# Four broadcast vectors out of four column tiles of one PSUM bank, with the order of all engines written anew

## The chip, the cores and the metric

The kernel runs on one core of one Trainium2 chip. The metric is the device time of one execution in microseconds (us); of several runs the median counts. The profiled execution and the plain runs are the same program.

## The reference, cut to what matters

A transformer block whose norms and residuals are modulated by a conditioning vector, on x of 2048 tokens by 512:

```python
mod = (silu(c) @ w_mod).reshape(1, 6, 1, 512)          # c: (1, 512)
sa, ca, ga, sb, cb, gb = mod[:, 0], ..., mod[:, 5]
h = layernorm(x) * (1 + ca) + sa
x = x + ga * A(h)      # 32 heads of 16, window of 256 tokens, qkv and output projections
h = layernorm(x) * (1 + cb) + sb
x = x + gb * B(h)      # layernorm, token-mixing MLP: 2048 -> 1792, gelu, 1792 -> 2048
```

Six vectors of 512 numbers come out of one small product. `sa` and `ca` are wanted along the partitions (`modFM`). The other four, `ga`, `cb`, `sb`, `gb`, are wanted as tiles of 128 equal rows, since tokens or MLP columns lie on the partitions where they are used: `bc_ga`, `bc_cb1` (cb + 1), `bc_sb`, `bc_gb`. These four are the subject here.

## The kernel before, in words

**Work.** The sequence is worked in four groups of 512 tokens. Of each group, queries, keys and values are projected (`pq`, `pk`, `pv`), heads are attended, the output is projected (`pa`, pieces named `wo`), added to x and normed twice (`l2`, `l3`) to give `hb`. Attention goes by 75 chunks: a score group on TensorE (`S`, names `pss` and `psb`), two exponentials on ScalarE (`et<-pss`, then `et<-psb`), masks on VectorE (`et<-et,maskt`), and on TensorE three pieces of weighted and plain sums (`po`, pieces named `AV`). `pss` has one buffer: the next score group waits for the exponential that reads it. The first MLP product runs in partial sums beside the last attention chunks (pieces `p`, names `pu`, `part`), the rest of it (`u`) after them, then the second product (`py`) and the output.

**Pieces.** Dense products are cut into pieces of two matmuls of 512 columns. A piece is emitted at full width, or as four column tiles of 32 columns of weights each (the helper `mm`); the scheduler picks the second where few dense pieces stand between sums (`NEAR_RUN`), so that TensorE need not change its tiling.

**Evictions.** Results in PSUM are taken out by VectorE or ScalarE (`qe` queries, `ke` keys, `ve` values, `pe` partial sums). [...]

**Order.** Nothing is left to run-time choice. `ops` lists all operations with their engines; `ORDER` is a table of numbers, the sequence in which they are emitted, and each engine runs its own in that sequence. `CHOSEN` names the operations that go to another engine than their first. `Ordered` pins the instructions of each queue, SyncE's transfers among them: an instruction that waits holds up all behind it on its queue.

**The place of the change.** `sT` is silu(c), four columns of 128. `sT_rep` spreads it to 4 x 128 equal columns, so that a matmul with it as weights gives 128 equal rows. For each of the four vectors `e_bc` runs four full-width matmuls of 512 columns into a bank of its own, and `e_bce` evicts that bank on VectorE into the tile, with the factor `ZSCALE` for `ga` and plus one for `cb`. `mod_ops` collects what must be done before the output projection: the four evictions, the MLP biases (`b12`, from the transfers `bl`) and the scaling of the output weights by `bc_ga` (`wod`). The loads of MLP weights (`w1`) wait for all of them too.

## Time and profile before

| | us |
|---|---|
| median of 3 runs | 258.86 |
| lowest and highest run | 256.61, 259.86 |
| time of the profiled execution | 257.62 |
| its span, first to last instruction | 255.8 |
| TensorE busy in the span | 240.1 |
| VectorE, ScalarE, GpSimd busy | 205.5, 172.8, 134.2 |
| TensorE's granted clock | 1.0 throughout |

The profiled execution takes 1.8 us more than its span, for what lies before the first and after the last instruction. Busy times are unions over an engine's instructions; matmuls overlap each other in the pipeline, so TensorE's figure is an upper one. Nearly all instructions carry line 254, that of the recording helper, so groups are told apart by the names of their tiles: `out<-in`.

### The profile page before, as it was taken

Reading aid. Unit: us, or ns where it says so; the run is one execution under the profiler, and the core shown is the slowest. Engines: PE = TensorE matmul, PEld = TensorE weight load, DVE = VectorE, ACT = ScalarE, POOL = GpSimd, SP = SyncE. Lnnn points to the kernel's source line nnn. Section 1 sums busy time; section 2 is a strip of 40 time slices with the busy share of each in tenths; the row PEclk is TensorE's granted clock in tenths of the full one; section 3 lists DMA queues with packets and bytes.
Section 4 is the critical chain, followed back from the end, with each engine's and each line's share of the span. In section 5 each row is a group of like instructions: output and inputs, shape, how many; then the busy total and the mean of one; then the engine's idle time right before and its main releaser. Section 6 shows DMA issues by size and latency. Waiting matters only on the chain.

```text
span 255.8 us, 11463 instructions
## 1 busy us (share of the span) xinstructions
PE 240.1 (94%) x5125; PEld 137.7 (54%) x5125; DVE 205.5 (80%) x378; ACT 172.8 (68%) x288; POOL 134.2 (52%) x220
## 2 busy tenths in 40 slices
PE   7999988999889889997999898999999999999995
PEld 3666655656656555655566455557444444444443
DVE  5599998999989979989798879898977974444443
ACT  4699998999998999997899898988207620000000
POOL 6069938967597599969787679964000000000000
PEclk9999999999999999999999999999999999999999
DMA  6998340381032100000621913401699901111111
GB/s 200 327 351 279 68 26 3 82 128 49 3 67 44 27 3 5 4 6 3 177 77 46 249 44 85 122 8 45 179 347 393 352 24 44 41 41 42 60 44 41
DMA packets 39657, 26.44 MB, mean 103 GB/s; under 512 B 11960, under 2 KB 35512, under 8 KB 39608
## 3 DMA queue, kind: packets, MB, share of 16 engines
q1 hardware_dynamic: 39600, 25.71, 35.4%
q8 instruction: 40, 0.66, 1.1%
q14 instruction: 9, 0.07, 0.1%
q10 hardware_dynamic: 8, 0.00, 0.0%
HBM read 22.03 MB, written 2.10 MB: 94 GB/s over the span
## 4 chain that ended last, share of the span: by engine, by line
PE 68%; DVE 16%; ACT 7%; issue 3%; DMA 2%; SPq 2%; POOL 1%; ACTq 0%
PE py L254 19%; PE pu L254 18%; PE po L254 8%; PE pss L254 7%; ACT et L254 7%; DVE et L254 5%; PE pa L254 4%; PE pk L254 3%; PE pq L254 3%; PE pv L254 3%; DVE h L254 2%; DMA x<-in_A_x_dram 2%; DVE st L254 2%; SPq L254 2%; DVE kb L254 2%
## 5 line engine op out<-in xcount | busy, mean ns | idle before, releaser
L254 ACT ACTIVATE et<-pss 128x1536 bf16<-128x1536 f32 (+2 forms) x90 | 101.5, 1147 | 12.0 <-PE psb L254 8.0
L254 PE MATMUL py<-guT,w2r 128*128 128x512 bf16 (+2 forms) x238 | 48.5, 366 | 0.0
L254 ACT ACTIVATE et<-psb 128x512 bf16<-128x512 f32 (+2 forms) x90 | 43.6, 508 | 0.0
L254 DVE TENSOR_TENSOR et<-et,maskt 128x2048 bf16<-128x2048 bf16 (+2 forms) x38 | 42.1, 1120 | 0.4 <-ACT et L254 0.4
L254 PEld LDWEIGHTS <-KT 32*128 32x128 bf16 (+1 forms) x1856 | 24.4, 97 | 30.4 <-issue 26.0
L254 PE MATMUL pu<-hb,w1s 128*32 128x512 bf16 (+1 forms) x260 | 38.8, 380 | 0.8 <-DVE part L254 0.7
L254 PE MATMUL pss<-QT,KT 32*64 32x32 bf16 (+7 forms) x1392 | 34.8, 202 | 4.8 <-ACT et L254 2.2
L254 PE MATMUL po<-et,VT 128*32 128x256 bf16 (+2 forms) x960 | 33.4, 234 | 3.8 <-DVE vb L254 2.2
L254 PEld LDWEIGHTS <-w2r 128*128 128x128 bf16 x238 | 22.8, 98 | 25.9
L254 PE MATMUL psb<-QT,KT 32*128 32x224 bf16 (+3 forms) x464 | 34.3, 203 | 0.9 <-issue 0.9
L254 PE MATMUL po<-et,ones_bd 128*32 128x256 bf16 (+3 forms) x624 | 31.4, 269 | 0.5 <-issue 0.5
L254 DVE TENSOR_TENSOR otile<-py,xr 128x512 bf16<-128x512 f32 (+2 forms) x17 | 11.2, 660 | 24.6 <-PE py L254 24.5
L254 POOL TENSOR_SCALAR KT<-kb,mask_par 128x512 bf16<-128x512 bf16 (+1 forms) x30 | 21.1, 714 | 13.2 <-DVE kb L254 11.8
L254 PEld LDWEIGHTS <-VT 128*32 128x32 bf16 x960 | 21.7, 96 | 10.8 <-issue 3.8
L254 DVE BATCH_NORM_STATS2 st<-x 128x6 f32<-128x512 bf16 x32 | 21.3, 680 | 2.0 <-DMA x<-in_A_x_dram 1.9
L254 POOL TENSOR_SCALAR VT<-vb,mask_half 128x512 bf16<-128x512 bf16 x25 | 20.1, 810 | 4.9 <-DVE vb L254 4.4
L254 PEld LDWEIGHTS <-w1s 128*32 128x32 bf16 (+1 forms) x260 | 13.9, 97 | 14.5 <-issue 1.2
L254 PE MATMUL pk<-h1T,wqkv 128*32 128x512 bf16 (+4 forms) x222 | 20.7, 333 | 0.0
L254 PEld LDWEIGHTS <-wqkv 128*32 128x32 bf16 (+1 forms) x380 | 15.2, 96 | 8.8 <-issue 1.1
L254 PE MATMUL pu<-hb,w1r 128*128 128x512 bf16 (+1 forms) x84 | 18.0, 380 | 0.0
L254 PE MATMUL pv<-wqkv,h1T 128*32 128x256 bf16 x512 | 17.6, 274 | 0.1
L254 PE MATMUL pa<-wod,OT 128*32 128x512 bf16 (+1 forms) x130 | 16.7, 381 | 0.2 <-DVE x L254 0.2
(107 smaller groups left out, 365.3 us busy)
## 6 DMA issues: line engine op xcount, KB each, us to landing
w2r<-in_B_w_dram SPq DMA_DIRECT2D x14, 512.0 KB, 10.5
w1s<-in_B_w_dram SPq DMA_DIRECT2D x19, 256.0 KB, 3.3
w1r<-in_B_w_dram SPq DMA_DIRECT2D x9, 256.0 KB, 4.9
x<-in_A_x_dram SPq DMA_DIRECT2D x16, 128.0 KB, 4.9
wmod<-in_w_mod_dram SPq DMA_DIRECT2D x4, 512.0 KB, 8.5
out_dram<-otile SPq DMA_DIRECT2D x15, 128.0 KB, 1.7
wmod<-in_w_mod_dram SPq DMA_DIRECT2D x4, 256.0 KB, 3.4
wqkv<-in_A_wqkv_dram SPq DMA_DIRECT2D x4, 256.0 KB, 5.2
```

The source lines that it names most:

```text
L254: ins = call(*args, **kwargs)
```

## The change

`sT_rep` keeps 32 equal columns instead of 128. One bank takes all four vectors: for each k the four matmuls write rows 0-31, 32-63, 64-95 and 96-127 from four column tiles. One eviction `bce` brings the bank to `bcs`, with a scale and an addend per partition (`bc_fix`: `ZSCALE` on the rows of `ga`, one added on the rows of `cb`). Four transfers on SyncE's queue (`bb`) then read the 32 rows of a vector four times over and fill the 128 rows of its tile. `ORDER` and `CHOSEN` are new tables.

```diff
 ORDER = [
-    2, 6, 0, 1, 7, 39, 8, 5, 40, 3, 9, 41, 10, 4, 42, 38, 11, 43, 13, 44, 45, 14, 46, 15, 47, 18, 16, 17, 20, 50, 48,
+    2, 6, 0, 1, 33, 7, 34, 8, 5, 35, 3, 9, 36, 10, 4, 37, 11, 38, 13, 39, 40, 14, 41, 15, 18, 42, 16, 20, 17, 19, 45,
...
 CHOSEN = {
...
-    sT_rep = modw.tile([P, ND, P], BF, name="sT_rep")
+    sT_rep = modw.tile([P, ND, 32], BF, name="sT_rep")
+    bcs = modw.tile([P, D], BF, name="bcs")
+    bc_fix = modw.tile([P, 2], F32, name="bc_fix")
+    nc.gpsimd.memset(bc_fix[:, 0:1], 1.0)
+    nc.gpsimd.memset(bc_fix[0:32, 0:1], ZSCALE)
+    nc.gpsimd.memset(bc_fix[:, 1:2], 0.0)
+    nc.gpsimd.memset(bc_fix[32:64, 1:2], 1.0)
...
-    o_rep = op("sTrep", "DVE", 0.35, lambda e: ve.tensor_copy(
-        out=sT_rep[:], in_=sT[:].unsqueeze(2).to_broadcast([P, ND, P])), deps=[o6], pos=-6, ready=15.0)
+    o_rep = op("sTrep", "DVE", 0.2, lambda e: ve.tensor_copy(
+        out=sT_rep[:], in_=sT[:].unsqueeze(2).to_broadcast([P, ND, 32])), deps=[o6], pos=-6, ready=15.0)
...
     mod_ops = []
-    for n, (v, dst) in enumerate(((2, bc_ga), (4, bc_cb1), (3, bc_sb), (5, bc_gb))):
-        def e_bc(n, v=v):
...
-                te.matmul(
-                    box["bc", v][:], lhsT=sT_rep[:, k, :], rhs=wmod[:, k, v * D : (v + 1) * D],
-                    start=(k == 0), stop=(k == ND - 1),
-                )
...
-        a, z = dense(f"bc{v}", [0.435] * 2, e_bc, [o_rep], 9.0 + n, cls="D", alloc="od", ready=22.0)
-        b = op(f"bce{v}", "DVE", 0.6, e_bce, deps=[z], pos=9.0 + n)
+    vectors = ((2, bc_ga), (4, bc_cb1), (3, bc_sb), (5, bc_gb))
+
+    def e_bc(n):
+        if n == 0:
+            box["bc"] = bank([P, D], F32, "ps_b")
+        for k in (2 * n, 2 * n + 1):
+            for i, (v, _) in enumerate(vectors):
                 te.matmul(
+                    box["bc"][32 * i : 32 * i + 32, :], lhsT=sT_rep[:, k, :], rhs=wmod[:, k, v * D : (v + 1) * D],
+                    start=(k == 0), stop=(k == ND - 1), tile_position=(0, 32 * i), skip_group_check=True,
                 )
...
+    def e_bce(e):
+        ve.tensor_scalar(
+            out=bcs[:], in0=box["bc"][:], scalar1=bc_fix[:, 0:1], scalar2=bc_fix[:, 1:2], op0=ALU.mult, op1=ALU.add,
+        )
...
+    for n, (v, dst) in enumerate(vectors):
+        def e_bb(e, n=n, dst=dst):
+            dma.dma_start(out=dst[:], in_=bcs[32 * n : 32 * n + 32, :].unsqueeze(1).to_broadcast([32, ND, D]))
+
+        mod_ops.append(op("bb", "SP", 0.65, e_bb, deps=[bce], pos=9.0 + n, extra=1.0))
```

What the tables move shows at three places.

VectorE, from the spreading of silu(c) to the first evictions of the vectors. Before (`ps_b` is the bank of a vector; `pk`, `pv` banks of projections, `et` exponentials):

```order
L254 COPY sT_rep<-sT 128x512
L254 CAST vb<-pv 128x512
L254 TENSOR_TENSOR et<-et,maskt 128x4x128
L254 TENSOR_TENSOR et<-et,maskt 128x4x64
L254 TENSOR_SCALAR KT_1_156<-kb,mask_par 128x8x32 x2
L254 TENSOR_TENSOR et<-et,maskt 128x8x64 x2
L254 CAST bc_gb<-ps_b 128x512
```

After the change:

```order
L253 COPY sT_rep<-sT 128x128
L253 TENSOR_TENSOR et<-et,maskt 128x4x128
L253 TENSOR_TENSOR et<-et,maskt 128x4x64
L253 CAST vb<-pv 128x512
L253 CAST kb<-pk 128x256
L253 CAST QT_1_148<-pk 128x256
L253 TENSOR_SCALAR KT_1_156<-kb,mask_par 128x8x32 x2
L253 TENSOR_TENSOR et<-et,maskt 128x8x64 x2
L253 TENSOR_TENSOR et<-et,maskt 128x4x128
L253 TENSOR_TENSOR et<-et,maskt 128x4x64
L253 CAST vb<-pv 128x512
L253 TENSOR_SCALAR bcs<-ps_b,bc_fix 128x512
```

One eviction stands a little later than the first of the four stood; the evictions of `bc_sb`, `bc_ga` and `bc_cb1` that followed it before are gone.

SyncE's queue behind the loads of x, before:

```order
L254 DMA_TRANSPOSE h1T_181<-xn 128x4x128 x4
L254 DMA b1b<-in_B_b_dram 128x14x1
L254 DMA b2b<-in_B_b_dram 128x16x1
L254 DMA w1s_1856<-in_B_w_dram 128x4x256
L254 DMA_TRANSPOSE h1T_180<-xn 128x4x128 x4
```

After the change:

```order
L253 DMA_TRANSPOSE h1T_181<-xn 128x4x128 x4
L253 DMA bc_gb<-bcs 128x1x512
L253 DMA bc_cb_118<-bcs 128x1x512
L253 DMA bc_ga<-bcs 128x1x512
L253 DMA bc_sb<-bcs 128x1x512
L253 DMA b1b<-in_B_b_dram 128x14x1
L253 DMA b2b<-in_B_b_dram 128x16x1
L253 DMA_TRANSPOSE h1T_180<-xn 128x4x128 x4
L253 DMA w1s_1957<-in_B_w_dram 128x4x256
```

The four transfers stand between the transposes of the second token group and the biases; the transposes of the third group now stand ahead of the first load of MLP weights instead of behind it.

ScalarE from the twelfth to the fifteenth chunk, before (`lz` are the logarithm and the reciprocal of the sums):

```order
L254 ACTIVATE et<-pss 128x3x2x256
L254 ACTIVATE et<-psb 128x2x256
L254 ACTIVATE lz<-lz 128x256
L254 ACTIVATE et<-pss 128x12x32 x2
L254 ACTIVATE lz<-po 128x256
L254 ACTIVATE et<-psb 128x4x32 x2
L254 ACTIVATE et<-pss 128x3x2x256
L254 ACTIVATE lz<-lz 128x256
L254 ACTIVATE et<-psb 128x2x256
L254 ACTIVATE et<-pss 128x3x2x256
```

After the change:

```order
L253 ACTIVATE et<-pss 128x3x2x256
L253 ACTIVATE et<-psb 128x2x256
L253 ACTIVATE vb<-pv 128x512
L253 ACTIVATE lz<-po 128x256
L253 ACTIVATE et<-psb 128x2x256
L253 ACTIVATE lz<-lz 128x256
L253 ACTIVATE et<-pss 128x12x32 x2
L253 ACTIVATE QT_1_152<-pq 128x512
L253 ACTIVATE et<-psb 128x4x32 x2
L253 ACTIVATE et<-pss 128x3x2x256
L253 ACTIVATE QT_0_151<-pq 128x512
L253 ACTIVATE et<-psb 128x2x256
```

Three evictions of projections (`vb`, twice `QT`) stand between the exponentials on ScalarE where none stood; they were VectorE's.

## The prediction

> **What bounds the kernel now.** I read the page's first two parts, then the chain of work that ended last, then busy time by stage.

> ```profile
> PE 240.1 (94%) x5125; PEld 137.7 (54%) x5125; DVE 205.5 (80%) x378; ACT 172.8 (68%) x288; POOL 134.2 (52%) x220
> PE   7999988999889889997999898999999999999995
> ACT  4699998999998999997899898988207620000000
> PE 68%; DVE 16%; ACT 7%; issue 3%; DMA 2%; SPq 2%; POOL 1%; ACTq 0%
> ```

> TensorE is on the chain for 68% of the span and wholly at the end; ScalarE is nearly full in the first 27 slices and then falls away. So there are two regimes, and I cut the span at the start of every tenth chunk, which is the start of its `et<-pss` exponential in ScalarE's timeline. First and last of these 75:

> ```profile
> 10.94 1.45 ACT L254 ACTIVATE et<-pss 128x1536 bf16<-128x1536 f32 x1 [0.73 <-PE pss L254]
> 173.32 1.44 ACT L254 ACTIVATE et<-pss 128x1536 bf16<-128x1536 f32 x1
> ```

> Busy time in these stretches (chunks 0-9, 10-19, and so on; then the tail of `u` pieces and the stretch of `py`); the columns are the length, then TensorE, weight loads, VectorE, ScalarE, GpSimd:

> ```profile
> 10.94:33.61 22.67, 21.59 (x564) 14.78 (x564) 22.08 (x53) 22.13 (x37) 16.69 (x32) 1.00 0.80 231
> 33.61:55.21 21.60, 19.33 (x665) 12.96 (x665) 20.61 (x40) 20.20 (x34) 15.01 (x24) 1.00 0.37 41
> 55.21:75.16 19.95, 18.73 (x588) 12.24 (x590) 18.41 (x31) 19.68 (x33) 15.49 (x26) 1.00 0.28 63
> 75.16:97.35 22.19, 19.28 (x684) 12.42 (x677) 20.71 (x35) 20.00 (x34) 17.70 (x26) 1.00 0.11 22
> 97.35:118.03 20.68, 20.08 (x630) 12.78 (x633) 18.60 (x30) 19.39 (x32) 18.23 (x26) 1.00 0.02 5
> 118.03:141.33 23.30, 21.84 (x606) 12.79 (x602) 20.51 (x33) 20.96 (x36) 19.21 (x24) 1.00 0.31 87
> 141.33:164.45 23.12, 21.43 (x573) 12.04 (x568) 19.80 (x30) 20.14 (x34) 18.98 (x25) 1.00 0.45 123
> 164.45:173.32 8.87, 8.87 (x206) 4.61 (x208) 8.39 (x17) 7.89 (x15) 6.58 (x12) 1.00 0.13 37
> 173.32:204.81 31.49, 31.49 (x305) 15.91 (x298) 26.90 (x60) 15.82 (x30) 2.02 (x2) 1.00 0.77 266
> 204.81:255.80 50.99, 48.38 (x238) 22.58 (x236) 23.92 (x38) 1.61 (x3) 0.00 (x0) 1.00 0.13 42
> ```

> Call them A to H, the tail, and the end. In A, VectorE and ScalarE are both full. In B and C ScalarE is within 1.4 and 0.3 us of the whole length, while TensorE is idle for 2.3 and 1.2 us. From E on TensorE leads, and in H and the tail it is never idle. The three engines hold each other:

> ```profile
> ACT et L254 <- PE psb L254: 8.0, 18, 1.2
> ACT et L254 <- PE pss L254: 3.4, 7, 1.1
> PE pss L254 <- ACT et L254: 2.2, 5, 0.7
> POOL KT L254 <- DVE kb L254: 11.8, 4, 7.2
> ```

> ScalarE waits 11.4 us in all for score groups, and a score group waits for ScalarE: one buffer, so that any eviction put between two exponentials can push the next score group, and the other way round.

> **The change, its own instructions.**

> ```profile
> L254 PE MATMUL ps_b<-wmod,sT_rep 128*128 128x512 bf16 x16 | 4.3, 382 | 0.0
> L254 DVE TENSOR_SCALAR bc_cb<-ps_b 128x512 bf16<-128x512 f32 x1 | 0.7, 676 | 0.0
> L254 DVE COPY sT_rep<-sT 128x512 bf16<-128x512 bf16 x1 | 0.4, 417 | 0.0
> 24.17 0.60 DVE bc_gb L254
> 26.64 0.68 DVE bc_sb L254
> 29.43 0.59 DVE bc_ga L254
> 47.45 0.86 PE pq L254 x16
> 49.22 0.98 PE pk L254 x4
> 107.83 1.10 PE po L254 x52
> ```

> TensorE: sixteen full-width matmuls cost 4.3 us busy. The chain has the price of the new form: sixteen column-tile matmuls of 512 columns (`pq` x16, the work of four) take 0.86. So a two-matmul piece is 0.43, eight pieces become two, and 6 x 0.43 = 2.6 us are saved (3.4 by the busy times). The same rows give the other prices: a sum piece is 1.10 / 3 = 0.37, and four matmuls at full width behind a score group are 0.98 instead of 0.86, so a change of tiling is about 0.12. Counted in the order, changes of tiling fall from 157 to 152: 0.6 us at most.

> [...]

> VectorE: four evictions at 0.68 become one, and the spreading at 0.42 shrinks to a quarter of its elements; that is between 0.10 and 0.42, taken as 0.15, near the small copies. Together 2.0 + 0.3 = 2.3 us less, all in A, where three of the four evictions stand on the chain at 0.59 to 0.68.

> GpSimd: four more small memsets at the start; it then waits 7.2 us for its first keys, which hides them. One of the like:

> ```profile
> L286 POOL MEMSET halves<- 128x4 f32 x1 | 0.1, 100 | 0.0
> ```

> The four transfers:

> ```profile
> 25.24 6.67 SPq L254 DMA_TRANSPOSE h1T<-xn  x4
> 31.96 0.57 SPq L254 DMA_DIRECT2D b1b<-in_B_b_dram  x1
> 1.72 1.85 SPq L254 DMA_DIRECT2D wmod<-in_w_mod_dram  x4
> L254 DVE TENSOR_TENSOR wod<-wod,bc_ga x4: 401/408/542, 37.9 to 48.3; 128x512 bf16<-128x512 bf16 x4
> x<-in_A_x_dram SPq DMA_DIRECT2D x16, 128.0 KB, 4.9
> out_dram<-otile SPq DMA_DIRECT2D x15, 128.0 KB, 1.7
> ```

> Four issues are 1.85 us on SyncE (`wmod` x4). They stand behind the transposes, so they go out from 31.9 to 33.8, and 128 KB land after 1.7 us (a quiet queue) to 4.9 us (a full one): 38.7 at the latest. The first reader is `wod`, now 37 rows behind `bcs` on VectorE; at some 0.6 us a row that is 22 us after an eviction at about 27, so near 49. Cost nothing, with 10 us of cover; without it VectorE would stand still for that long in the worst case, and everything behind `wod` with it. The biases go out 1.9 us later, still far ahead of their reader beside `wod`. The transposes of the third group are now ahead of the MLP loads, no loss.

> **The change, what the tables move.** This decides more than the vectors do. Counted in the order, dense pieces between score groups go from 20 to 30 in B, from 25 to 26 in E, and fall by 2 in F, 4 in G, 2 in H and 3 in the tail; sum pieces fall by 2 in D, rise by 2 in E and 1 in F, fall by 1 in G. Evictions on ScalarE rise by 4 in B, 1 in C, 2 in E, 1 in F and fall by 1 each in A and the tail; VectorE has six operations more in B, GpSimd sixteen instead of eight there. The price on ScalarE:

> ```profile
> L254 ACT ACTIVATE part<-pu 128x512 f32<-128x512 f32 x2 | 1.2, 588 | 3.1 <-PE pu L254 3.1
> ```

> Stage by stage, against the rows above:
> - A: VectorE falls to 19.8; ScalarE has one eviction less, 22.1 - 0.6 = 21.5, and is the bound now. Gain 0.6 (nothing to 2.3).
> - B: TensorE 19.33 + 10 x 0.43 = 23.6; ScalarE 20.20 + 4 x 0.59 = 22.6; VectorE 20.61 + 6 x (0.41 to 0.68) = 23.1 to 24.7. The stage was 21.60; I take 23.9, the middle of VectorE's bounds: loss 2.3 (2.0 to 3.1).
> - C: ScalarE 19.68 + 0.59 = 20.3: loss 0.3.
> - D: TensorE has 0.7 less but does not lead: nothing (to 0.7 gained).
> - E: TensorE 20.08 + 0.43 + 0.74 = 21.25, and the stage lay 0.6 above it: loss between 0.6 and 1.2, taken 0.9.
> - F: 0.37 - 0.86: gain 0.5.
> - G: 4 x 0.43 + 0.37 = 2.1 of TensorE's time; with ScalarE at 20.1 and VectorE at 19.8 below it I take 1.5 (nothing to 2.1).
> - H: 0.86, TensorE never idle there: gain 0.9.
> - Tail: 3 x 0.43: gain 1.3. The end is unchanged, the same 238 matmuls.

> Sum: -0.6 + 2.3 + 0.3 + 0.9 - 0.5 - 1.5 - 0.9 - 1.3 = -1.3 us. The profiled execution takes 257.62, so 256.3; the median of the runs lies 1.24 above that execution, so the forecast for a median is 257.6. Most of the 2.6 us saved on TensorE is spent in B, where work was pulled forward into a stage that three engines now fill.

> **The rivals.**

> 1. The early stages take the work without strain. For it: TensorE's 2.3 us idle in B, VectorE's relief in A on the chain, and ScalarE's 11.4 us of waiting. Against it: B's counts. Then A gains 2.3, B loses 2.0, C nothing, D gains 0.7, E loses 0.6, F to the tail gain 0.5, 2.1, 0.9, 1.3, tilings 0.6: -5.8, that is 253.1.

> 2. ScalarE's loop becomes the bound: evictions between exponentials push the score groups, and what TensorE no longer has to do in F and G turns to idle time instead of gain. For it: ScalarE at 20.2 of 21.6 in B and 19.7 of 19.95 in C before it gets five more. Against it: ScalarE is idle for 2.3 and 3.0 us in F and G. It decides when B takes more than its busiest engine, as D does (22.19 for 20.71, 1.5 more). GpSimd's doubled work in B helps it:

> ```profile
> L254 POOL TENSOR_TENSOR h<-h,bc_sb x5: 1157/2016/2055, 118.1 to 163.6; 128x512 bf16<-128x512 bf16 x5
> ```

> The same operation takes from 1157 to 2055 ns there, so work on GpSimd can stretch while others run, and keys and values for the next chunks come from it. Price: B 24.7 + 1.5 = 26.2, loss 4.6; C 1.3; E 1.2; A, F and G nothing; H and the tail gain 0.4 and 0.9: +5.8, that is 264.7. [...]

> 3. The vectors don't come cheaper: either the four column tiles run one after the other (2.6 us back, 260.1), or a transfer holds `wod`. Against it: `pq` x16 at 0.86 in the chain, and 10 us of cover.

> **How the numbers follow.** Forecast 0.56, first rival 0.14, second 0.24, third 0.06. The predicted time is the forecast's, 257.6. The range reaches to both rivals, 252.8 to 265.0; the forecast's own bounds are 254.0 to 260.8, from A, B, D, E and G all at their ends. Faster by over 2% (below 253.7) holds the first rival: 0.13. Slower by over 2% (above 264.0) holds most of the second: 0.22. Within 2%, which is about what a measurement of this kernel can tell from no change: 0.65.

> **What would show it.** Right: `ps_b` busy near 1.1 us in one place, `bcs` once on VectorE at 0.67, the four transfers out near 32 us and no wait for them at `wod`; A about 22, B near 24, G near 21.6, the tail near 30.2; ScalarE's evictions of 0.6 us between exponentials in B. Wrong: B above 25.5 us or F and G as long as before (second rival); B below 22.5 with A near 20.5 (first); VectorE idle ahead of `wod`, or `ps_b` busy for 3 us and more (third). If H or the tail have idle time on TensorE, a late norm or load has taken its place, and the sum fails there.

## The result and the profile after

The changed kernel takes 260.54 us in the median of 20 executions (258.20 to 262.46), the kernel before 257.45 in as many beside it. The ratio is 1.0109, with a 95% interval of 1.0083 to 1.0134: slower by 1.1%, inside the range of the forecast and within the 2% that it gave 0.65, but on the other side of no change than the forecast had it. The ratio leaves out the executions that lie over 1.5% above the fastest of their kernel, so it is not quite that of the medians. The profiled execution takes 261.64 us with a span of 259.9, 4.1 more than the span before.

Four lines of the page of the changed kernel: TensorE's busy time, the slices of ScalarE and of the granted clock, and the shares of the chain that ended last.

```profile
PE 240.5 (93%) x5161; PEld 139.1 (54%) x5161; DVE 206.2 (79%) x381; ACT 177.1 (68%) x294; POOL 119.0 (46%) x212
ACT  4497899988989999999999989999216720000000
PEclk9798899999999999999999999999999999999999
PE 54%; ACT 16%; POOL 11%; DVE 11%; issue 4%; DMA 2%; SPq 1%; DVEq 0%; POOLq 0%; ACTq 0%
```

ScalarE has 4.3 us more, GpSimd 15.2 less, TensorE as much as before. TensorE's share of the chain fell from 68% to 54%; what it lost went to ScalarE (7% before) and GpSimd (1%). The clock dips in two places.

Busy time by stage, cut as before at every tenth chunk (length, then TensorE, weight loads, VectorE, ScalarE, GpSimd, and the granted clock):

```profile
12.56:37.42 24.86, 20.22 (x636) 14.92 (x633) 20.31 (x50) 21.72 (x36) 15.08 (x29) 0.93 0.69 199
37.42:62.05 24.63, 23.25 (x712) 15.14 (x715) 22.94 (x44) 22.93 (x38) 21.32 (x34) 1.00 0.37 58
62.05:83.38 21.33, 18.91 (x636) 12.33 (x636) 19.77 (x35) 19.98 (x32) 16.14 (x25) 1.00 0.58 90
83.38:104.51 21.13, 18.14 (x593) 11.76 (x593) 19.64 (x34) 20.31 (x35) 17.81 (x25) 1.00 0.02 3
104.51:126.69 22.18, 21.25 (x636) 13.25 (x638) 20.65 (x35) 21.15 (x35) 11.01 (x18) 1.00 0.14 40
126.69:148.37 21.68, 21.47 (x620) 12.87 (x616) 18.61 (x31) 21.02 (x35) 13.80 (x22) 1.00 0.38 102
148.37:169.88 21.51, 19.98 (x534) 11.40 (x528) 19.89 (x32) 19.98 (x33) 11.28 (x16) 1.00 0.23 62
169.88:177.87 7.99, 7.97 (x204) 4.37 (x206) 7.56 (x15) 7.79 (x15) 6.55 (x13) 1.00 0.14 38
177.87:208.94 31.07, 31.05 (x301) 15.33 (x292) 27.11 (x59) 16.17 (x30) 1.42 (x1) 1.00 0.77 271
208.94:259.90 50.96, 48.05 (x237) 22.42 (x235) 23.68 (x38) 1.01 (x2) 0.00 (x0) 1.00 0.13 42
```

Against the rows of before:

| | lead | A | B | C | D | E | F | G | H | tail | end | sum |
|---|---|---|---|---|---|---|---|---|---|---|---|---|
| forecast | 0 | -0.6 | +2.3 | +0.3 | 0 | +0.9 | -0.5 | -1.5 | -0.9 | -1.3 | 0 | -1.3 |
| measured | +1.62 | +2.19 | +3.03 | +1.38 | -1.06 | +1.50 | -1.62 | -1.61 | -0.88 | -0.42 | -0.03 | +4.10 |

The lead is the time to the first exponential. The last cut lies 0.2 us behind the first `py` matmul before and 0.5 behind it after; cut at that matmul itself (204.64 and 208.45), the tail is 0.74 shorter and the end 0.27 longer. The two largest surprises stand at the start. A row of TensorE's timeline in the changed kernel:

```profile
24.22 1.15 PE L253 MATMUL pv<-wqkv,h1T 128*32 128x256 bf16 x24 [1.49 <-issue]
```

And windows of 1 us (the clock is the third figure from the end, then the share of the transfer engines):

```profile
8.00:9.00 1.00, 1.00 (x12) 0.54 (x11) 0.23 (x2) 0.00 (x0) 0.00 (x0) 0.50 1.18 332
25.00:26.00 1.00, 1.00 (x26) 0.54 (x22) 1.00 (x5) 0.00 (x0) 0.87 (x2) 0.50 0.16 46
27.00:28.00 1.00, 1.00 (x20) 0.47 (x16) 0.00 (x0) 1.00 (x2) 1.00 (x2) 0.50 0.00 0
```

TensorE stands still for 1.49 us in the middle of a `pv` piece, waiting for nothing that the profile shows ("issue"), and then its clock is 0.50 for 3.4 us (24.6 to 28.0); it is 0.50 once more from 7.5 to 11. The profiled execution of before has neither.

The vectors themselves did nearly what was forecast. Four rows of the views by tile, and one of the transfers' landing times:

```profile
L253 PE MATMUL ps_b<-wmod,sT_rep x16: 379/525/634, 27.1 to 28.2; 128*32 128x512 bf16 x16
L253 DVE TENSOR_SCALAR bcs<-ps_b,bc_fix x1: 810/810/810, 28.6 to 28.6; 128x512 bf16<-128x512 f32 x1
L253 SPq DMA_DIRECT2D bc_cb<-bcs x1: 1252/1252/1252, 34.7 to 34.7; - x1
L253 DVE TENSOR_TENSOR wod<-wod,bc_ga x4: 415/418/419, 51.9 to 55.9; 128x512 bf16<-128x512 bf16 x4
```

```profile
bc_cb<-bcs SPq DMA_DIRECT2D x1, 128.0 KB, 3.3
```

One place, 27.1 to 28.6, mostly at half clock; one eviction, of 0.81 us for the 0.67 forecast; transfers out from 33.9 to 37.2, two us later than forecast; the landings on record took 2.7 to 3.3 us, the last at 39.3. `wod` first reads 12 us later and does not wait.

### The profile page after: what moved, and what is told of

Read it like the earlier page. It is cut to its first block, busy times and chain, and to the rows that moved or that the text cites. A ratio compares the mean times of both kernels' runs of the same rounds, so it can differ in the third digit from the quotient of the medians.

```text
span 259.9 us, 11550 instructions
## 1 busy us (share of the span) xinstructions
PE 240.5 (93%) x5161; PEld 139.1 (54%) x5161; DVE 206.2 (79%) x381; ACT 177.1 (68%) x294; POOL 119.0 (46%) x212
## 4 chain that ended last, share of the span: by engine, by line
PE 54%; ACT 16%; POOL 11%; DVE 11%; issue 4%; DMA 2%; SPq 1%; DVEq 0%; POOLq 0%; ACTq 0%
PE py L253 19%; ACT et L253 14%; PE pu L253 13%; PE pss L253 7%; PE po L253 6%; PE pa L253 4%; POOL sq L253 2%; DVE et L253 2%; DVE st L253 2%; DMA wmod<-in_w_mod_dram 2%; DVE h L253 2%; PE pv L253 2%; POOL rs L253 2%; POOL KT L253 2%; ACT lz L253 1%
## 5 line engine op out<-in xcount | busy, mean ns | idle before, releaser
L253 PEld LDWEIGHTS <-KT 32*128 32x128 bf16 (+1 forms) x1856 | 25.0, 97 | 32.9 <-issue 29.2
L253 PE MATMUL pu<-hb,w1s 128*128 128x512 bf16 (+1 forms) x242 | 39.2, 380 | 0.5 <-DVE OT L253 0.4
L253 DVE TENSOR_TENSOR et<-et,maskt 128x2048 bf16<-128x2048 bf16 (+2 forms) x38 | 38.9, 1038 | 0.6 <-ACT et L253 0.3
L253 DVE TENSOR_TENSOR otile<-py,xr 128x512 bf16<-128x512 f32 (+2 forms) x17 | 11.2, 660 | 24.5 <-PE py L253 24.4
L253 PEld LDWEIGHTS <-VT 128*32 128x32 bf16 x960 | 20.7, 96 | 7.9 <-issue 1.2
L253 POOL TENSOR_SCALAR KT<-kb,mask_par 128x512 bf16<-128x512 bf16 (+1 forms) x28 | 19.2, 699 | 11.6 <-DVE kb L253 11.4
L253 PEld LDWEIGHTS <-w1s 128*128 128x128 bf16 (+1 forms) x242 | 13.9, 97 | 16.1 <-issue 2.0
L253 PE MATMUL pk<-h1T,wqkv 128*32 128x256 bf16 (+4 forms) x282 | 21.2, 317 | 0.2
L253 POOL COPY et<-et 128x512 bf16<-128x512 bf16 x16 | 11.4, 720 | 19.0 <-ACT et L253 18.5
L253 POOL TENSOR_SCALAR VT<-vb,mask_half 128x512 bf16<-128x512 bf16 x23 | 16.3, 717 | 2.0 <-ACT vb L253 2.0
## 6 DMA issues: line engine op xcount, KB each, us to landing
x<-in_A_x_dram SPq DMA_DIRECT2D x16, 128.0 KB, 5.0
out_dram<-otile SPq DMA_DIRECT2D x15, 128.0 KB, 1.7
```

Source lines behind the costliest of these rows:

```text
L253: ins = call(*args, **kwargs)
```

## The experiments

All ratios are to the kernel before, run beside them. "Idle" is the sum of TensorE's idle times of 0.25 us and more that the profile puts down to "issue", in the profiled execution; B is the length of that stage there. Both are of one execution each.

| kernel | ratio, 95% interval | idle | B |
|---|---|---|---|
| before | 1 | 3.00 | 21.60 |
| the change | 1.0109 (1.0083 to 1.0134) | 2.94 | 24.63 |
| e1 new vectors, old order | 1.0026 (0.9994 to 1.0059) | 3.14 | 21.29 |
| e2 new order, old vectors | 1.0337 (1.0292 to 1.0382) | 5.10 | 25.79 |
| e3 change, early pieces full width | 1.0055 (1.0019 to 1.0091) | 1.36 | 25.37 |
| e6 old kernel, early pieces as tiles | 1.0135 (1.0092 to 1.0177) | 4.94 | 21.26 |
| e4 change, five evictions back on VectorE | 1.0119 (1.0079 to 1.0158) | 3.77 | 26.30 |
| e5 change, second norm later | 1.0179 (1.0128 to 1.0230) | 3.65 | 27.17 |
| e7 change, lighter norm | 1.0041 (1.0006 to 1.0076) | 5.42 | 24.79 |
| e9 e1 and idle matmuls | 0.9928 (0.9896 to 0.9959) | 0.49 | 20.26 |
| e10 old kernel and idle matmuls | 0.9958 (0.9929 to 0.9987) | 0 | 21.15 |
| e11 e1 and narrow idle matmuls | 0.9971 (0.9938 to 1.0004) | 0.31 | 20.43 |
| e12 old kernel and 24 idle rows | 0.9927 (0.9891 to 0.9962) | 0.31 | 22.82 |
| e16 old kernel and 120 idle rows | 0.9966 (0.9936 to 0.9995) | 0 | 20.72 |
| e13 e3 and idle matmuls | 1.0119 (1.0061 to 1.0177) | 2.02 | 24.92 |
| e14 e3 and 60 idle rows | 1.0146 (1.0101 to 1.0191) | 4.74 | 27.23 |
| e15 e3 and 120 idle rows | 1.0221 (1.0165 to 1.0276) | 4.77 | 26.77 |

**Vectors or order?** e1 is the changed kernel with the old tables: the new pieces stand where two of the old ones stood. e2 is the old kernel with the new tables.

```diff
 e1, on the change
-ORDER, CHOSEN = the new tables
+ORDER, CHOSEN = the old tables; bc at the places of bc5, bce at bce5's, bb behind the fourth load of x
 e2, on the kernel before
-ORDER, CHOSEN = the old tables
+ORDER, CHOSEN = the new tables; each bcN, bcN, bceN beside the score group it stood at
```

> The new way to make the four vectors, in the order that the kernel before had: the two pieces stand where the first vector's two pieces stood, the one eviction where the first eviction stood, the four transfers right behind the transposes of the second token group, and every engine choice is the old one. Theory A (the new tables cost the time, the vectors themselves are cheap): 1 to 2.5 us faster than before, ratio 0.990 to 0.997, with the stage of the first ten chunks about 1 to 2 us shorter than 22.7 and no wait of VectorE ahead of wod. Rival B (the vectors themselves cost, by the wait for the one bank, the slower eviction of 0.81 us and the transfers): 1 to 3 us slower, ratio 1.004 to 1.012, and the first ten chunks longer.

> The order and the engine choices of the changed kernel, but the vectors made the old way: four times two full-width pieces and an eviction, each three put as one block near the chunk at which it stood before. Theory A: slower than the changed kernel by 1 to 3 us, so ratio 1.014 to 1.022 over the kernel before. Rival B: equal to the kernel before or up to 1 us over it, ratio 1.000 to 1.004.

e1 came out between the two theories' ranges, with an A of 23.74 us (longer, not shorter): the vectors alone change nothing that these runs can tell. e2 is slower than expected. So the loss is not the vectors'. It comes with the tables, and in their order the old vectors, put there in blocks that nobody tuned, cost still more.

**The gap at 24 us.** With the new tables six query and key products of four matmuls (two pieces each) ahead of the seventh score group are emitted as four column tiles, with four times the matmuls: 72 more, five of the products in one run of 80 matmuls where 20 stood, in the same time (2.37 us; the 20 take 2.36 in e3). e3 forces them to full width in the change; e6 forces tiles on all such early products of the old kernel, eleven of them, 132 matmuls more.

```diff
 e3, in run_schedule
+    groups = 0
+    for i in ORDER:
+        groups += ops[i].name == "S"
+        if groups <= 6 and ops[i].name in ("q", "k"):
+            ops[i].tiled = False
 e6, the same on the kernel before, with
+            ops[i].tiled = True
```

> The changed kernel, except that the query and key pieces ahead of the seventh score group are emitted at full width (two matmuls) instead of as four column tiles (eight). Theory C (early column tiles quadruple TensorE's instructions, so that TensorE runs dry near 23 us for 1.5 us, and the granted clock then falls to one half for about 3.6 us): the wait of 1.5 us for issue ahead of pv is gone, the clock stays at 1.0 between 20 and 30 us, and the time is 1.5 to 2.5 us below the changed kernel's, ratio 1.002 to 1.006 over the kernel before. Rival D (the gap comes from the loads that fill the transfer engines, or by chance): gap and clock as in the changed kernel, ratio 1.009 to 1.013.

> The kernel before with its q and k pieces ahead of the seventh score group computed as four column tiles in place of full-width matmuls, as the changed kernel does; order and vectors stay the old ones. Theory I (early column tiles make TensorE outrun the supply of its instructions while the loads fill the transfer engines): a gap of 0.8 to 1.6 us opens before a boundary of 256 instructions between 21 and 25 us, where the kernel before has none, stage A takes 23.5 to 25 us (22.67 before), and the ratio is 1.003 to 1.010. Rival W (the gap belongs to the changed order's other contents, a late weight or a wait that the profile shows nothing of): no gap over 0.4 us before 30 us, A within 0.5 us of 22.67 or lower by the shorter steps, ratio 0.997 to 1.002.

In e3 the gap is gone and the ratio falls from 1.0109 to 1.0055, inside theory C's range (the two intervals just overlap); the clock, which theory C wanted at 1.0 up to 30 us, still fell at 28.7. In e6 the gap appears, larger, where the old kernel has none; stage A grows from 22.67 to 26.57, 2.53 of it the gap, and all three figures lie beyond theory I's ranges; a row of TensorE's timeline in e6 and its stage A, then A and B of e3:

```profile
22.67 1.05 PE L261 MATMUL pk<-h1T,wqkv 128*32 128x256 bf16 x30 [2.53 <-issue]
```

```profile
11.19:37.76 26.57, 21.64 (x680) 15.06 (x681) 22.74 (x53) 22.68 (x38) 18.64 (x33) 1.00 0.78 192
```

```profile
11.28:34.58 23.30, 20.44 (x564) 14.77 (x563) 20.60 (x50) 22.18 (x36) 15.31 (x28) 0.93 0.82 223
34.58:59.95 25.37, 23.01 (x709) 15.17 (x715) 22.59 (x44) 22.95 (x38) 21.68 (x34) 1.00 0.45 63
```

The matmul behind the gap is the same one in the program's count in both, row 704 of TensorE's order (a weight load and its matmul are two rows); in the change it is `pv`, in e6 `pk`. So it hangs on a number of rows, not on an operation. The kernel before has such gaps too, at rows 1724, 4282, 4794, 6070 and 7862:

```profile
40.71 0.29 PE L254 MATMUL po<-et,VT 128*32 128x192 bf16 x8 [0.68 <-issue]
83.44 0.38 PE L254 MATMUL po<-et,ones_bd 128*32 128x256 bf16 x5 [0.48 <-issue]
91.44 0.17 PE L254 MATMUL psb<-QT,KT 32*64 32x32 bf16 x1 [0.60 <-issue]
112.04 0.17 PE L254 MATMUL psb<-QT,KT 32*64 32x32 bf16 x1 [0.32 <-issue]
146.41 0.20 PE L254 MATMUL pss<-QT,KT 32*64 32x32 bf16 x2 [0.92 <-issue]
```

Modulo 256 these are 182 to 188. Counted by the weight loads in the traces, all 63 such idle times of the seventeen kernels lie at 182 to 194 modulo 256. The page's queue of instructions moves about as many rows in a packet:

```profile
q8 instruction: 40, 0.66, 1.1%
```

40 packets for 10322 rows in the trace, that is 258 rows and 16.4 KB each; from the first packet to the last TensorE goes through 251 rows a packet in the change and 254 before. Below, a block is 256 rows, and a boundary the place in each at which these idle times lie. TensorE passes most boundaries without a wait (63 idle times for some 680 packets in seventeen executions), but one cost 2.53 us.

The traces' transfer records point to what TensorE waits for. 57 of the 63 idle times end 1.2 to 1.6 us after a packet of this queue has landed, the other six 1.7 to 2.3 us after: in the change the packet sets out at 21.67, lands at 22.81, and TensorE goes on at 24.22. Behind each of the 63 the next packet sets out only 1.0 to 2.9 us after TensorE has gone on, so no further block was on its way while it waited. The packet of 21.67 set out 4.5 us after the boundary before (near row 448, passed at 17.2), and 3 to 5 us after it in all seventeen kernels, where the transfer engines' share is 1.1 from 17 to 21 us. That the loads held it up is likely, but not shown.

**What bounds B?** e4 puts the five evictions that the tables gave to ScalarE in chunks 9 to 24 back on VectorE, e5 moves GpSimd's second norm four chunks later, e7 cuts eight instructions of a norm to three, leaving out its real statistics.

```diff
 e4, in CHOSEN["ACT"]
-274, 277, 301, 304, 530
 e5, in ORDER
-the second norm aggregate at chunk 15
+the second norm aggregate at chunk 19
 e7, in the norm's statistics
+            if key == ("l1", 3, 0):
+                po.tensor_tensor(out=mv[:], in0=st[:, :, 1:3], in1=st[:, :, 4:6], op=ALU.add)
+                po.tensor_tensor(out=rs[:], in0=halves[:, 0:n, 1], in1=power[:, 0:n], op=ALU.pow)
+                po.tensor_tensor(out=nm[:], in0=halves[:, 0:n, 1], in1=rs[:], op=ALU.mult)
+                return
```

> The changed kernel with the five evictions that its tables moved to ScalarE in chunks 9 to 24 given back to VectorE; nothing else differs. Theory G (GpSimd's second norm and what it feeds sets the end of stage B): ScalarE is not what B waits for, so B stays at 24.3 to 25.2 us and the ratio to the kernel before at 1.009 to 1.016, since VectorE takes the 3 us that ScalarE loses. Theory S (ScalarE's exponentials and evictions are the bound of B, my rival 2): B falls by 1.5 us or more, to 23.1 or less, and the ratio to 1.002 to 1.006. Either way the gap of about 1.5 us before the matmul 351 of TensorE stays.

> The changed kernel with one operation of GpSimd moved: the statistics of the norm of the last token group (eight small instructions, 4.7 us in the changed kernel's trace) stand five operations later in GpSimd's queue, behind the keys, values and h1T of the third token group, four chunks later. Theory E (GpSimd is the bound of chunks 10 to 19, where it got sixteen operations for eight): that stage falls from 24.6 us to 22 to 23.5, and the time is 1 to 2 us below the changed kernel's, ratio 1.003 to 1.007 over the kernel before. Rival F (the four evictions on ScalarE and the ten pulled-forward dense pieces bound that stage): the stage stays above 24 us, ratio 1.009 to 1.013.

> The changed kernel with GpSimd's statistics of the last token group's norm cut from eight instructions to three; the real statistics of that group are left out. Some 3 us of GpSimd's work in stage B go, nothing else moves. Theory G (GpSimd's queue of the two norms, the normalised tokens and their transposes sets the end of B): B falls to 23.2 or less (24.63 in the changed kernel), the ratio to 1.001 to 1.006. Theory S (ScalarE is the bound): B stays at 24.2 to 25.2, the ratio at 1.009 to 1.014. The gap before the matmul 351 stays in both.

Stage B of e4, then of e7:

```profile
34.80:61.10 26.30, 23.74 (x709) 15.32 (x715) 25.18 (x48) 21.15 (x35) 21.91 (x34) 1.00 0.32 57
```

```profile
36.66:61.45 24.79, 23.33 (x709) 14.95 (x715) 23.93 (x44) 23.20 (x39) 20.44 (x30) 1.00 0.35 62
```

e4: ScalarE has 1.8 us less, VectorE 2.2 more, and B is 1.7 longer, above the ranges of both theories. ScalarE alone is not the bound (theory S fails); VectorE cannot take the work either. e7: GpSimd has 0.9 less, not the 3 expected, and B is as long as in the change, with 0.68 us of idle time at a block boundary in it that the change has not; the ratio lies in theory G's range, B in theory S's. Its profiled execution is a long one (262.70 us, median 259.53), but neither of its dips of the clock falls in B. e5 missed: the norm moved, and VectorE's normalising steps, which wait for it (2.49 us, until 58.4), now stand ahead of other work in VectorE's queue; with two things changed it tells nothing on GpSimd alone.

The chain that ended last tells more. In the change it lies on GpSimd for 18.4 of B's 24.63 us, from the norms over the keys and values of the next chunks to the end of the stage; three of its pieces:

```profile
42.77 1.19 POOL sq L253
59.15 2.55 POOL KT L253 x2
61.70 1.38 POOL VT L253 x2
```

Before, no part of B's chain lay there. In e7 it is VectorE for 16.3 us and B, without its idle time, is only 0.5 us shorter; in e3, with the same tables, TensorE has the largest part (11.2). So GpSimd set B's end in the change, with the others close behind: taking work from one engine alone brought little. TensorE, VectorE and ScalarE are busy for 93 to 94% of B there, GpSimd for 87%. Which of them sets the length in other executions is not shown.

**Is it the work of TensorE or the place of the boundaries?** e9 to e12 and e16 add matmuls whose result nobody reads, at the places of three old vector pieces.

```diff
 e9, on e1: six half pieces into a bank of their own
+                te.matmul(box["bd", v][:], lhsT=wmod[:, k, 0:P], rhs=wmod[:, k, v * D : (v + 1) * D], ...)
 e11, the same with 32 columns
+                te.matmul(box["bd", v][:, 0:32], lhsT=wmod[:, k, 0:P], rhs=wmod[:, k, v * D : v * D + 32], ...)
 e10, e12, e16, on the kernel before: zeros added to the vectors' sums
+                if v != 5 and k == 2 * n:
+                    for _ in range(2):      # 10 in e16
+                        te.matmul(box["bc", v][:, 0:32], lhsT=nothing[:, 0:P], rhs=nothing[:, 0:32], ...)   # 0:D in e10
```

> The changed vectors in the old order, as in the first experiment (ratio 1.0026), and beside them at the places of the three pieces that the change saves six half pieces of two full-width matmuls each, whose result nobody reads. Theory K (the vectors themselves save time, but TensorE's shorter or emptier work in the first 30 us lets its clock fall to 0.5 for some 3.5 us more often, which takes the gain away): most executions run at a mean clock of 1.000 and the ratio is 0.995 to 1.000 although TensorE does 2.6 us more work. Rival N (the clock's dips do not hang on this work): the same share of executions below 1.000 as in the first experiment (8 of 12), and the ratio is 1.002 to 1.010, since the idle matmuls cost what they take.

> The kernel before, vectors and order as they were, with twelve idle matmuls (zeros, 128x512) added inside the six half pieces of bc2, bc3 and bc4: 24 more rows of TensorE's program, 2.6 us more of its work in stage A. Theory P (what the ninth experiment gained is the phase: rows are supplied in blocks of 256, the 24 rows move every later block boundary off the places where the program runs through its rows fastest): TensorE's idle times of 0.25 us and more that wait for nothing the profile shows add up to under 1.0 us after 35 us (3.0 us in the kernel before), stage A is up to 1.0 us longer, ratio 0.990 to 0.999. Theory W (the gain was the vectors'): the idle times stay near 3 us and the ratio is 1.000 to 1.008.

> The ninth experiment (changed vectors, old order, idle matmuls) with the twelve idle matmuls narrowed from 512 columns to 32: the same 24 rows, but nearly none of the work. Theory P (phase of the blocks of 256 rows): TensorE's unexplained idle times after 35 us stay under 0.6 us as in the ninth experiment (2.1 us in the first), ratio 0.988 to 0.996. Theory K (the filled time of TensorE and with it the clock): they may go, but the clock falls as often as in the first experiment (8 of 12 executions below 1.000) and the ratio is back at 0.999 to 1.006.

> The kernel before with twelve narrow idle matmuls (zeros, 128x32) inside the half pieces of bc2, bc3 and bc4: only 24 rows more in TensorE's program, nothing else differs. Theory P: the idle times at rows 1724, 4282, 4794, 6070 and 7862 of TensorE's program (0.68, 0.48, 0.60, 0.32 and 0.92 us in the kernel before) go or shrink to under 1.0 us in sum, stages B, D, E and G get shorter by about these, ratio 0.987 to 0.996. Theory W (the ninth experiment's gain was the vectors') and theory K (it was the filled time): both 0.999 to 1.004 here.

> The kernel before with 120 narrow idle rows in place of 24. Theory P (the phase of the 256-row blocks decides): idle times at rows 182 to 194 modulo 256, at other places of the program than before; the ratio follows their sum, about 0.992 plus 0.004 for each us of it (0.9927 with 0.3 us, 1.000 with 3.0), so 0.990 to 1.004. Rival Z (any idle rows help, by the time they take or give): 0.990 to 0.995 with no regard to the sum of the idle times.

e9 came out below the ranges of both theories, on K's side, but e12 shows that K is not the main reason: with nothing but 24 narrow rows the old kernel gains as much. e10 keeps theory P's ratio and idle time, though its A takes 1.9 us more, not 1.0. e11 falls between: its idle time goes, as P said, and its clock is below 1.000 in 7 of 12 executions, as K said. Stages D to G of e12:

```profile
76.81:98.24 21.43, 19.52 (x684) 12.35 (x677) 20.68 (x35) 20.00 (x34) 16.93 (x26) 1.00 0.17 23
98.24:118.46 20.22, 19.94 (x630) 12.77 (x633) 18.39 (x30) 19.40 (x33) 18.15 (x26) 1.00 0.02 5
118.46:141.75 23.29, 21.83 (x606) 12.76 (x602) 20.51 (x33) 20.96 (x36) 19.19 (x24) 1.00 0.32 87
141.75:163.81 22.06, 21.36 (x573) 12.04 (x567) 19.70 (x30) 20.14 (x34) 18.98 (x25) 1.00 0.48 130
```

D, E and G are shorter than before by 0.76, 0.46 and 1.06, and the gaps that stood there were 1.08, 0.32 and 0.92; F, which had none, is unchanged. Its B is 22.82 because this profiled execution has a dip of the clock at 38 to 42 us. All five kernels with the old tables and shifted boundaries lose nearly all idle time and lie at 0.993 to 0.997. Within these five the ratio does not follow the last tenths of idle time, so theory P's slope in e16 is only roughly right (0.9966 for 0.992); rival Z's range was missed too.

The vectors' own worth can be read here at equal boundaries: e9 against e10 is 0.3% faster, e11 against e12 is 0.4% slower, e1 against the kernel before 0.3% slower. No two of these are told apart by their intervals: some 3 us of instructions saved on TensorE and 2 on VectorE bring nothing measurable.

**Are the new tables slower by themselves?** e13, e14 and e15 take e3 and add idle rows in chunks 6 to 10, as e9, e11 and e16 did for the old order.

```diff
 e13, on e3: the six half pieces of e9 in chunks 6, 8 and 10
 e14, e15: the same six half pieces of 5 and 10 narrow matmuls each
+            for m in range(5 * n, 5 * n + 5):      # 10 in e15
+                te.matmul(box["bd", v][:, 0:32], lhsT=wmod[:, 0, 0:P], rhs=wmod[:, 0, 0:32], ...)
```

> The changed kernel with both faults mended: its early q and k pieces full width (as in the third experiment) and twelve idle full-width matmuls of 512 columns, 24 rows and 2.6 us of TensorE, in chunks 6 to 10. Nothing is left out. Theory T (the new tables only move work from F, G, H and the tail into B, where three engines are then full, so they bring nothing of their own): no gap of 0.25 us and more at 24 us, the others under 0.7 us in sum, executions mostly at full clock, and yet B takes 24.2 to 25.5 us and the ratio to the kernel before is 0.999 to 1.006, 1.005 to 1.012 above the ninth experiment's 0.9928. Rival O (the order is the better one and lost only by the gap and the clock): ratio 0.985 to 0.994, as low as the ninth experiment or lower.

> The changed kernel with full-width early pieces and 60 idle rows (30 matmuls of 32 columns) in chunks 6 to 10. Theory T (the tables themselves are slower, since they move work into B): whatever idle time at block boundaries is left, B stays at 24.2 us or more and the ratio is 1.000 to 1.010. Theory O (only the boundaries' places were against the new order): if the unexplained idle time is under 0.8 us, the ratio is 0.988 to 0.997.

> As the one before, with 120 idle rows. Theory T: B at 24.2 us or more, ratio 1.000 to 1.010. Theory O: with under 0.8 us of unexplained idle time 0.988 to 0.997.

Theory T holds on B (24.92, 27.23, 26.77), theory O's low ratios never came. But I expected the idle time to fall and it rose: 2.0 to 4.8 us against 1.36 in e3, and in all three the ratio lies above T's range as well. A row of TensorE's timeline in e13, its stages B and C, then B of e14:

```profile
77.11 0.40 PE L260 MATMUL pv<-wqkv,h1T 128*32 128x256 bf16 x6 [1.06 <-issue]
```

```profile
35.44:60.36 24.92, 23.11 (x712) 14.98 (x711) 22.58 (x43) 22.95 (x39) 21.68 (x34) 1.00 0.39 67
60.36:83.28 22.92, 20.62 (x640) 12.72 (x638) 20.55 (x36) 19.97 (x32) 18.34 (x27) 0.93 0.37 84
```

```profile
34.80:62.03 27.23, 23.19 (x709) 15.12 (x715) 23.30 (x43) 23.41 (x38) 22.51 (x35) 1.00 0.44 62
```

In the new order stage B has 712 matmuls in place of 665 before. Without the idle times in it, B takes 24.6 to 25.4 us in the five kernels of the new order whose engine choices and norms are the change's (the change, e3, e13, e14, e15), against 20.9 before and 20.3 to 21.2 in e9, e10, e11 and e16. The cleanest pair is e3 and e9, the same vectors in the new and the old order without the early gap: 1.0055 against 0.9928, and B is 25.37 without any idle time of this kind, against 20.26. Stage B of e9, to be read beside that of e3 above:

```profile
34.93:55.19 20.26, 18.59 (x664) 12.88 (x654) 18.89 (x37) 19.99 (x34) 15.23 (x23) 1.00 0.52 59
```

B is 5.1 us longer in the new order for 4.4 us more of TensorE, 3.7 of VectorE, 3.0 of ScalarE and 6.4 of GpSimd. The stages from F to the tail give back 4.7 of it, but C and E take 2.4 more beyond their idle times. So the tables are slower by themselves, by some 1%.

## Why the prediction was wrong, point by point

- **What bounds the kernel, and the vectors' prices.** Right: one place, one eviction, no wait at `wod`, where the cover took up transfers that went out two us late; the third rival was not met. The spreading of silu(c) took 0.50 us in this order (0.22 in e1) for the 0.15 taken. That most of TensorE's saving would be spent again was right as well.
- **A, -0.6 forecast, +2.19 measured: this step failed.** ScalarE bounds A as forecast (21.72 us busy for 21.5, and the chain lies on it for 16.4). But I priced a column-tile piece at 0.43 us, the same work as at full width, and looked only at busy time. It also has four times the rows. Six such early products, five of them in a row, bring TensorE to the boundary at row 704 by 22.73 us, before the next packet of instructions has landed (22.81): 1.49 us, and in this execution a dip of the clock behind it (e4, with the gap and no dip, has an A of 23.89). Undone (e3) the kernel gains half a per cent; done to the old kernel (e6) it costs 1.35%.
- **The lead, +1.62, was not forecast.** It is a dip of the clock at 8 us in this one execution. The other sixteen have leads of 10.8 to 11.4, so it belongs to the profiled span and not to the change.
- **B, +2.3 forecast, +3.03 measured.** The mechanism was right in part, the size too small: the counts gave the loads (TensorE 23.25 for 23.6, ScalarE 22.93 for 22.6, VectorE 22.94 for 23.1 and more), but with the engines that full the stage takes 1.4 us more than its busiest, and 0.68 us of the old B had been idle time at a boundary, so that the tables' own cost there is 3.7. My second rival said "more than its busiest engine" and named ScalarE for it; e4 shows that it was not ScalarE alone. A term was missing: I counted GpSimd's operations there (sixteen for eight) and priced none. They took 21.32 us for 15.01, and the chain of B lies on them. What GpSimd lost in E, F and G (7.2, 5.4 and 7.7 us) had no price either.
- **C, +0.3 and +1.38.** 0.86 of it is a gap at row 3770. **E, +0.9 and +1.50**: right in kind, too small.
- **D, 0 and -1.06; G, -1.5 and -1.61.** D's whole difference is idle time at boundaries, 1.08 us before and none after, so the work there changed nothing, as forecast. G had 0.92 of it before and 0.59 after: some 1.3 us are the pieces moved out, and the match with 1.5 is close but not exact. What a boundary alone can do there e12 shows, whose G is 1.06 us shorter with the old tables.
- **F, -0.5 and -1.62; H, -0.9 and -0.88; the tail, -1.3 and -0.42.** F gave more, and why is not shown. The tail gave less (0.74 by the better cut): TensorE is never idle there, as forecast, but three pieces less did not show in full.
- **The sum.** Both profiled executions have the same idle time at boundaries (3.00 and 2.94), so it cancels in the total, though not in the stages. Without it the stages from A to the end sum to +2.5 instead of -1.3: A 0.7 (the dip), B 3.7, C 0.5, E 1.8, then F -1.6, G -1.3, H -0.9, tail -0.4. The failed terms are A, B, E and the tail; F's miss, the other way, hid part of it. The base was off too: I put the median 1.24 us above the profiled execution from three runs, and twenty runs of the kernel before put it 0.17 below. None of the signs that I had listed for the rivals came in the change (B stayed below 25.5, F and G got shorter): a sum of many terms can fail without any rival.

What stays open: what sets A's length in the old order, where it takes 23.67 and 23.82 us with the new vectors (e9, e11) and 22.99, 24.15 and 24.53 with the old (e12, e16, e10), so that the runs show no cost or gain of the vectors there; what sets B's length besides the load; and what gives GpSimd's lighter norm its 0.7% while B stays as long.

## What to carry to other kernels

Count instructions as well as busy time: here a piece split in four tiles cost the same matmul time and four times the rows, and TensorE stood still for 1.49 us at a boundary of its program, until 1.4 us after a packet of instructions had landed. Price every engine of a stage, also the one that was far from the chain before. Read idle time put down to "issue" in the middle of a piece by its row number; if the rows share a remainder, a few idle rows early in the program move all later boundaries and may be worth more than the edit at hand: here 24 rows gained 0.7% on the tuned kernel, as much as the best version with the new vectors (e9). Work pulled forward into a stage whose engines were nearly all 90% busy was paid there in full and more, and most of it came back later, but not all.

## What the runs showed of the hardware that was not expected

```profile
L253 POOL TENSOR_SCALAR sq<-sq x9: 203/203/1227, 23.9 to 172.6; 128x4 f32<-128x4 f32 x9
```
